# Output stores from SyncE's queue, and a new order of work, in a fused S4 convolution and SwiGLU kernel

## The chip, the cores and the metric

The kernel runs on one core of a Trainium2 chip, as one program. The metric is the device time of one execution in microseconds (us), as a median of runs. The core has TensorE (PE; its weight loads are shown as PEld), VectorE (DVE), ScalarE (ACT), GpSimd (POOL) and SyncE (SP), each with an instruction queue of its own that is worked off in order, and 16 DMA engines. DMAs are issued from SP's queue and, for some transfers, from ACT's; an engine issues a DMA as an instruction in its queue and does not wait for it to land.

## The reference

The input `x` (2048 rows of 512) is normalized row by row. Two branches start from the result: a state space convolution over the rows (S4: a filter of length 2048 for each of the 512 channels, made from 128 complex modes, applied through Fourier transforms) and a SwiGLU feed-forward layer (512 to 1792 to 512). The output adds their product to `x`.

```python
def _A_ref(u, A_re, A_im, B_re, B_im, C_re, C_im, log_dt, Dskip):
    ...
    P = jnp.exp(logdA[:, :, None] * l[None, None, :])
    K = jnp.einsum("dn,dnl,dn->dl", Cc, P, dB).real
    ...
    Yf = Uf * Kf[None, :, :, :]
    y = irfft2(Yf)[..., :L] + u * Dskip
def _B_ref(x, w_gate, w_up, w_down):
    g = _silu(x @ w_gate)
    u = x @ w_up
    return (g * u) @ w_down
x = A_u
xn = _layernorm(x, axis=-1)
s = _A_ref(xn, ...)
g = _silu(_B_ref(xn, ...))
return x + s * g
```

## The kernel before, in words

**A planner and a written-out order.** The kernel function does not emit instructions directly. It describes 1966 tasks by `add(engine, duration, function, rd, wr, up, ...)`: a task is one or a few instructions of one engine, with the buffers that it reads (`rd`), writes (`wr`) or fills a part of (`up`). The string `LIST` holds the order in which the tasks are emitted, two characters a task. `Plan.run` goes through the tasks in that order, gives each a time by its own durations, and from these times derives three things: where each buffer lies in one SBUF arena (`place`) and in eight PSUM banks, which DVE and POOL tasks are kept apart (`part_ports`), and where TensorE gets filler products while it would be idle (`keep_warm`, emitted at line 1439). Then the tasks' functions are called in list order; the framework adds the semaphores. So each engine works its own tasks in the order of the list, and the list sets the order of everything.

**The stages.** They overlap in the list.

- The head: `x_load`, `ln_group`, `x_norm` load tiles of `x` (xt), compute mean and rstd, centre and scale them, split them into two 16-bit parts (xh) and transpose them on PE (line 540, into xT). `w_load`, `w_norm`, `w_scale_gu`, `w_split` load the weights in chunks, square and sum them on ACT (line 604), and split each chunk into a high 16-bit part (ACT, line 669 or 666) and a low one (DVE line 670 or POOL line 667).
- The feed-forward layer: `half_mm` (line 699, 24 products of 256 columns a task, 16-bit) for gate and up, `ffn_unit` (ACT lines 720 and 724, DVE 722 and 725) and `down` (line 741, six products of 512 columns). SiLU of the result (zg, lines 750 and 753) is kept in SBUF, or for the first ten tiles in DRAM (zg_d).
- The filter: `prep`, `batch`, `kg_tables`, `kg_trig`, `kg_prod`, `kg_mm` (line 1150) and `kg_s1` (line 1183) make the filter and its first transform; it goes to DRAM as `ak_d`.
- The transforms: `x_stage1` (line 563) writes `ax_d`; `s2_load`, `s2_mm`, `s2_prod`, `s2_inv` load `ak` and `ax`, multiply them, transform back and write `bs_d` (DRAM, line 1295), for two halves of 256 channels.
- The end: `final` does the last transform of a pair of row tiles and one half of the channels, or of one row tile and all channels (the last two, 14 and 15). It loads `bt` from `bs_d` (by `load`, line 468), `fx` from `x` (line 1315), and for the first ten tiles `fz` from `zg_d`; PE makes `py` (line 1330), DVE multiplies by zg (1349 or 1337), DVE or POOL adds `fx` (1354, 1352 or 1338) and two DMAs store the result `ot`, one for each half of the partitions. A tag like `ot6_1` is the pair that begins with tile 6, second half of the channels; `bt15_1` is tile 15.

**Which queue stores.** A pair's two stores (128 KB each, 28 in all) are issued by ACT, and of the four stores of tile 14 and of tile 15 (64 KB each) two by SP and two by ACT:

```python
for h in range(2):          # tiles 14 and 15, line 1340
    add(("SP", "ACT")[h], 0.6, ... (sy, nc.scalar)[h].dma_start(ov[h, :, j0, sl], ot...), rd=[ot], ...)
...
for h in range(2):          # pairs, line 1356
    add("ACT", 0.6, ... nc.scalar.dma_start(ov[h, :, j0:j0 + nj, cs], vw(ot)...), rd=[ot], ...)
```

All other DMAs, but two halves of the first tiles of `x`, are issued by SP: 280 tasks of SP before.

Of the kernel before, what the change touches and what calls it, by code (L numbers as in the profile page):

```python
# [46 lines left out]
LIST = (
    "###$#(#'#%#&#K#J#L#)#D#T#.#M#i#k#l#U#V#W#Y#N#P#X#/&0#m#O#R#j#n#o#Z#Q#S#1#2#q(*#4#5#*#v#p#w#r#x&+#y(+(,#s$&(.#t#+"
    "$'#z$($)#{#[#,#-#](-${%Q#}#:$##_&A#d#^#e(/#|(0(4#f&3#`#8#g$*#a#;#b#7&.$-&/#C&:#<#h&1&,&5$$#c$}$.(:(6#9$w$x$1$y%%"
    "(1&B$+$z&?%.#?&z$2$3&;&<$/#=(5(7(<&=$=#0$<$;$4&6$,$>$5&D(@(8(L(9%&%'%<(F#A$6(;%$(A$F$?$Q$7(R#>$S$8$@%/$A#u%R$B$C"  # L50
    "$H&8$G(S$I$|(G%2$9(B$:(H(I(C(_(2$J$K#@$R$T(N(`#B(T&H(M#I&@#3$N$k%##6&F$b$U$L(D(=%T(O$V$M$Y$](X(>$D$E$%$O$P&G(e(3"
    "(J&9(P(U(Q(V(K#F(Y(Z(?([$0$^$W$X$Z$[(E&E&J(](^&V$e$n(W(g(a%($q$_$`(b%+$a$c#E(q&u(r(})#)$$t%7&C$f%8%9(k(f(w$g$d)("
    ")=)>(m%)(c(h(d(i)%%-%*%B%,)R)S&I$h%A(j%U&K)&(y$u%C(l$v$l$m%D$i(n&W%5$o$j$r)T(x$p)))0&k&X)1)?)F%E%Y%=%>(z%G%?$s&l"
    "%6&L&M&N&m&-({(|%0)U)2%F)]%H(o(p%:&a&b&c%1%@&Y%I%J)3%;(s%K-H)G%3%4%L%M&O&Z%N)H-I-M%O(t-N)I)'(u&d)J(v&e&n&o):);&P"
    ")^&4&Q&T&p&s&f&[&q-J-K&i-L&_&]-O-P&g&y'$-W%S-X&t-^)b)i)j)k-m)_)*-T-Q&j-Y&`-n&R-[-V-`-R)K-S)l-_-e-f)<-U)s)t)@-Z)+"
    "&v&})`-v&7-x-{&S)c-t-u&^-w-z-a&h-c),-b-g)B-i-d&2&>)A-h-q-o-s-p.6.7.8.9.:.;)a.<-])d-j)4&r.#.&.')-.%).)/)6)5#H)u.)"
    "-r)L)7.(.*-|.=%P-k-l-y)N)8.>)C)9-})D%Z&U.$.+.Y)E.A.C.?.@)V.B.F)w.H.K.D.E.G)x.,.-%V%`)W)M.../)v.I.1.J.L.M)m.0.2.3"
    "%a.Z.4.O)X.g)O.N.P.S)e.U)y)n.Q.R.[.T.5.]&w%[)o&x)f%d)g.h)h/$/%/&)Y)P)Q)p)z.c.p.^._.e.V.W.X)Z/#*$.`*%)[%W%X%n*1.i"
    ".j.l*2){)|.k.m.a.b/'/(*&*'*()q)r*.%].n/).o.d.q.r**%i*/.f.s%j%k*3/+)}.t.u*:*).v%_*+*,*4*#/*'#.w*0.y/./,/-%l*-.x.z"
    ".{%o%p*5%e&{%b%f*6/7/0/3/5%c.|.}&'%^%t*7/8*;*B//*C*F/F/1/9/2/:%s/4/<%m*<%u&|*8/;/=/S*=*G/6*D/H/I*E*9/G/@/>/B/?%v"  # L60
    "*H*I/T/A/M*>/N%w/K*L/P*M*N*?*O/l/m/n'%'S*@*A*T'&/k%q%r*J*P*Q*K/O/J/C/o/]/p*U*V&)*R/Z/[/L%y/U*S/Q/_/q/V*W/^/r*X%g"
    "/W'''(*Y/X0W')0Y*h/Y03'1'2/D/E*Z*]*^/t/u/R'3/`*['*'+/s/a/b'E'F'4'5*e*f/y*o%x/w/c/f/d%z%{*i0$#G';/g*j/e','/'-'6'9"
    "/z'7'0'G/h'./v*_':*`&#&$%|*k0%&%%}/x/{%h/}*l/|&*'T&&&(0@'80&*a'H*p'I'<'=0#040+0X0,*q*b0'0)*c*d*m*n/j'P0Z0A0.0D0-"
    "0709*w*x*r0(0*0/0F'O+$0B+%'>'?000<0>05+.06080[0:+/'J0C0E*s*g0;0=0I0K0102'U/i'M0]*t0^0_0G0H'@'A0`0a'C0b'D0c+00J'W"
    "*u*v0d+&'N0l0?0L*y0p0n110e0j0k0m'K0M0N+'+60g0i0f0h'V*z'Z0O0S'Y0Q0q*{1%0o0R0t0y0v0P0T+(+10w0x*|1$0z1:*}+#120{0V1+"
    "1,1.1&1'+)1(+2+3+4+50U1H1*+*+7+81)+++:0r0s0u0|1-'L1I+,1J1K'R'q1/10+-1314+>160}1#+9+;151L1M1N1P'Q'X'[18+?19+@171O"
    "+B'{+I'g1<+P1;+<+=1='B1Q1V1W1X1^1Y+A+C1]'h'i1>+Q1?+D1z1R1Z+X1T+Y1f1h+F1S'|'}'r's1U+a+G1@+H1D+J1B1l']'^'_1C1y1d1e"
    "1g'j(#'k1A1E1a($+b1m2627281_1c1`+L1{1|+R1b+E1n1o2#1G+K+M1p'`1['a1q25+N1i+O2''t2)'u+S+T1u1w1j1k1F1s1t'b+U+c29+d+Z"
    "1r+]'c2%2&2(1v+V+W2:1}2$2;2<'d2='v+['e'l(%2I2C2D'w1x'o'p(('y()2F2J2*+^2+2,+e2@2B2X2E2G(&2>2?2A(''z2Y+_'x'f+k+l+`"
    "+s2H2K2f+g'm'n2L2N2M2O2R+m+t2g3#2`+f2T2a2P3$2Q+h2b2Z2S2[2d2]2^2U2_+u2}2c3j3l+i+j+w2o3k2V+{2W2q2j2l2h2i+v2k+x3&3y"  # L70
    "3'2m3(+n2n2p2-2/213x+o+y+z3w+p2e2r483%2.20222423+q+r3m3}2s2t3p3n3o3r3q3t3)3s3z3*3{3|4#+|4%4&+}4$3u,#,(372u2w4'30"
    "4`,*,1,22v2x2y2z2{3v,$31334(2|3234363-3/3+3,3.,)384)4*3S,+,%4+,&,'474^3540413E,343443F464-4.393;4E3=3>3?3A3:3R,,"
    "3<4m,9,-3G3@,43H3J4/3B3L49,:,A3I3K,B3N3P3M3O4C4D3C3D3Y3V3X3Z3]4_3T4,3U3W4;3Q3[3^4<4:4=,.73,C4F4>4G4H4I4J4?5*4@4A"
    "4l3_3`3a4k4M4a454c4b,/,54B5,3b3c4L3e,;573d,<,03f3g593h424d4K4g4n4p4o4O4N,D5+4f,E,J,6,74h4e4j4P3i,8,K4Q4R5:4q4Z4["
    ",=585;4u4s4t4r5-,>4v4W4X4w5w,?,@,F,G4i4T4]4U5<5=5A5?4Y4S5.5/50545>5@5B,L,M,R5x6A4x,H5$4|52535Q51564y556(,N4z4{5%"
    "4V,S,T,O5',P6)5y5{5z,I4}5C5#,Q5(5|6$,U5)6B6*6,6+5&5^,Z,[6#6%5}6'6-606.6&616/626C6D6E,V72,W5R635S5T5_5U6F6H6J6G5`"
    "6I6K6g7X,X,Y5a,],^6h6N5b5D6L5H5I5J,e,l5E5F5G5N5O5P5K5L5M,m5c5f5g5e5d6i6j6k7V,t5h6M5i,c646t,d5V65667=67,f6s6>6?,g"
    "6O6Q6P5X5W6R5Y5Z5[5]6l6S6V6T6@6U6X6W,h8=7C71,_68696:6o6n6;6p6u6v6w6<7:74,u6m6r6=6x6|6z6{7L6y8+758)7F,|7G,n,i,j6q"
    "6}7W7i7#,`,},a8W7h,b765j7}7N-#,v7O,k5k5l7U,o5t5u5n7$5o5q5r5s5m7%7E8X7&,p847(7)7.,w7j777+6Y6Z7*7/7D7,7-6d,x6a7k6b"
    "6c6e6f-*-+7'8D6[5v7a6^-$5p,q70,r6]6_,y,z7r,s6`-,7_--7Y7Z7[82,{7P8E8:7`8c8(8;7]-.-/8f-08d7t7z-%-&-'8C-(-2-3-4-6-5"  # L80
    "-)8U817H-7-8-98V-17;7b787d8,7M7^7<-:8>8*7c7e-?7f8-7m7Q7I7K7q8<7s-@-A8N7J8?7R7>-;-<838e-=-B8L7?7@7B7|8F7S8H7T7l7n"
    "8G8@7{7o->8A8I8K8J8M-C8Y8Z8[7u8^-D-E-F85-G8_8#7g7v7p8O8.807A8B8/868`8b8a798P7w8Q8$7y7x87888g8h8]8i8k8l8j8m8o898n"
    "8R8S8T8%8&8'"
)
LIST = [DIGITS.index(a) * 90 + DIGITS.index(b) for a, b in zip(LIST[::2], LIST[1::2])]
ROOM = 103.0 * 1024
# [306 lines left out]
def kernel(  # L393
# [904 lines left out]
    def final(js, cs, c):  # L1298

        nj, nd = len(js), cs.stop - cs.start  # L1300
        j0 = js[0]
# [31 lines left out]
        if nj == 1:  # L1333
            for q, z in enumerate(zgs[j0]):
                ot = buf(f"ot{tag}{q}", 1024, "ot")
# [3 lines left out]
                for h in range(2):  # L1339
                    add(("SP", "ACT")[h], 0.6, lambda h=h, ot=ot, sl=sl: (sy, nc.scalar)[h].dma_start(ov[h, :, j0, sl], ot.f32()[h * 64:(h + 1) * 64]),  # L1340
                        rd=[ot], up=[key("out")], c=0, dma=dma_us(65536, 64), pr=pr)
            return
        ot = buf(f"ot{tag}", 2048, "ot", int(W["c_ot"] + 0.5))
        e = pr
# [8 lines left out]
        else:  # L1353
            add("DVE", 0.7, lambda: V.tensor_tensor(ot.f32(), ot.f32(), fx.f32(), op=ALU.add), rd=[fx], wr=[ot], c=1, pr=e, port=True)
        for h in range(2):
            add("ACT", 0.6, lambda h=h: nc.scalar.dma_start(ov[h, :, j0:j0 + nj, cs], vw(ot)[h * 64:(h + 1) * 64]), rd=[ot], up=[key("out")], c=0,
                dma=dma_us(131072, 64 * nj), pr=e)


# [127 lines left out]
```

## Time and profile before

| | |
|---|---|
| median of 3 runs | 598.75 us (598.53 to 599.48) |
| profiled execution | 597.17 us, its span 595.4 us |
| mean granted TensorE clock | 0.992 |
| PE busy | 578.9 us (97%), 7626 products |
| DVE, ACT, POOL busy | 428.6, 343.3, 325.8 us |
| DMA | 90.48 MB, mean 152 GB/s |
| queue of SP, of ACT | 85.12 MB, 4.20 MB |
| output stores: ACT line 1356, ACT 1340, SP 1340 | 28, 4, 4 |

How to read the views: the page's first part gives each engine's busy time; products on PE are pipelined, so a busy PE is not yet a PE at its peak. The stretches (a view by windows) give busy times, granted clock and DMA share in a part of the span. The chain of waits follows the work that ended last back from the end; a row is start, length and what it was. The timeline lists instructions in order of time, those of one kind merged (x5 is five of them, the second number the time that they took together); ACTq and SPq are DMA issues on the queue of ACT and of SP, and idle time before an instruction stands in brackets with what ended it. The view of one line gives the least, median and greatest duration in ns, and the time from a DMA's issue to its landing.

### The profile page before, as it was taken

How to read it: one execution, taken by the hardware profiler on the slowest of the kernel's cores; microseconds unless marked ns; L12 is line 12 of the kernel's file. 1: busy time of each engine (PE TensorE's matmuls, PEld its weight loads, DVE VectorE, ACT ScalarE, POOL GpSimd, SP SyncE). 2: the span in 40 equal slices, each digit the busy share in tenths (PEclk: the TensorE clock that was granted, in tenths of full speed). 3: DMA queues.
4: the chain of work that ended last, by engine and by line, in shares of the span. 5: the costliest groups of instructions: out<-in, count | busy, mean ns of one | idle time of the engine just before them, and what ended most of it. 6: DMA issues, size and time to landing. Idle time of an engine off the chain costs nothing.

```text
span 595.4 us, 18328 instructions
## 1 busy us (share of the span) xinstructions
PE 578.9 (97%) x7626; PEld 410.6 (69%) x7626; DVE 428.6 (72%) x992; ACT 343.3 (58%) x699; POOL 325.8 (55%) x301
## 2 busy tenths in 40 slices
...
GB/s 267 250 307 255 191 89 0 11 179 92 20 77 14 30 98 29 59 73 134 107 90 38 19 108 143 137 153 184 248 212 203 253 271 259 241 259 291 256 259 174
DMA packets 99762, 90.48 MB, mean 152 GB/s; under 512 B 38432, under 2 KB 84256, under 8 KB 99680
## 3 DMA queue, kind: packets, MB, share of 16 engines
q1 hardware_dynamic: 95168, 85.12, 49.5%
q10 hardware_dynamic: 4512, 4.20, 2.8%
...
## 4 chain that ended last, share of the span: by engine, by line
PE 92%; ACT 3%; issue 1%; DVE 1%; DMA 1%; SPq 0%; POOL 0%; POOLq 0%; ACTq 0%
PE p L699 48%; PE p L741 25%; PE p L1150 5%; PE p L1243 3%; PE p L1236 3%; PE p L1330 3%; PE p L1283 2%; PE p L563 1%; PE p L1183 1%; PE p L540 1%; DMA wd<-in_B_w_gate_dram 1%; ACT wu L604 1%; ACT wg L669 1%; PE p L799 1%; ACT wg L604 0%
## 5 line engine op out<-in xcount | busy, mean ns | idle before, releaser
L699 PE MATMUL p<-arena,wu 128*128 128x256 f16 x1344 | 154.7, 273 | 1.9 <-issue 1.8
L699 PE MATMUL p<-arena,wg 128*128 128x256 f16 x1344 | 155.0, 273 | 0.1
L741 PE MATMUL p<-wd,arena 128*128 128x512 f16 x672 | 154.2, 379 | 0.0
L699 PEld LDWEIGHTS <-wu 128*128 128x128 f16 x1344 | 130.0, 98 | 24.2 <-issue 7.5
L699 PEld LDWEIGHTS <-wg 128*128 128x128 f16 x1344 | 129.1, 98 | 25.0 <-issue 5.9
L741 PEld LDWEIGHTS <-arena 128*128 128x128 f16 x672 | 63.8, 98 | 73.8 <-issue 5.6
L1083 POOL TENSOR_TENSOR arena<-arena 128x1536 f32<-128x1536 f32 x32 | 90.7, 2842 | 25.4 <-ACT arena L720 6.2
L1075 POOL TENSOR_TENSOR arena<-arena 128x1024 int32<-128x1024 int32 x32 | 62.5, 1957 | 24.6 <-DVE arena L531 7.2
L720 ACT ACTIVATE arena<-p,inv 128x512 f32<-128x512 f32 x56 | 37.9, 685 | 46.3 <-PE p L699 41.3
L722 DVE SCALAR_TENSOR_TENSOR p<-p,shc,arena 128x512 f32<-128x512 f32 x56 | 41.9, 754 | 25.4 <-PE p L699 19.9
L724 ACT CAST arena<-p 128x512 f16<-128x512 f32 x56 | 32.5, 588 | 43.6 <-DVE p L722 40.4
L1118 DVE TENSOR_TENSOR arena<-arena,p 128x512 f32<-128x512 f32 x64 | 43.5, 680 | 6.3 <-ACT arena L567 2.6
L1265 POOL TENSOR_TENSOR arena<-arena 128x512 f32<-128x512 f32 x16 | 20.4, 1275 | 47.6 <-PE p L1236 14.3
L1098 ACT ACTIVATE p<-arena 128x512 f32<-128x512 int32 x64 | 38.7, 608 | 12.6 <-POOL arena L1075 5.6
L725 DVE TENSOR_TENSOR arena<-p,arena 128x512 f16<-128x512 f32 x56 | 37.7, 681 | 10.0 <-ACT arena L724 9.9
L1352 POOL TENSOR_TENSOR arena<-arena 128x512 f32<-128x512 f32 x12 | 15.0, 1268 | 51.5 <-DVE arena L1349 39.5
L1099 ACT ACTIVATE p<-p,halfpi 128x512 f32<-128x512 f32 x64 | 42.2, 664 | 1.5
L1100 ACT ACTIVATE p<-arena 128x512 f32<-128x512 int32 x64 | 37.6, 606 | 5.6 <-DVE arena L1120 3.2
L1124 DVE SCALAR_TENSOR_TENSOR arena<-arena,p 128x256 f32<-128x256 f32 x64 | 26.4, 413 | 18.7 <-POOL arena L1083 11.8
L1253 ACT COPY arena<-p 128x512 f32<-128x512 f32 x32 | 17.4, 591 | 31.0 <-PE p L1236 30.9
L1150 PEld LDWEIGHTS p<-arena 128*32 128x32 f32 x2048 | 29.7, 110 | 6.7 <-issue 4.4
L1150 PE MATMUL p<-arena 128*32 128x64 f32 x2048 | 33.6, 220 | 0.0
...
## 6 DMA issues: line engine op xcount, KB each, us to landing
...
ak_d<-arena SPq DMA_DIRECT2D x16, 512.0 KB, 5.8
arena<-ak_d SPq DMA_DIRECT2D x16, 512.0 KB, 4.5
arena<-ax_d SPq DMA_DIRECT2D x16, 512.0 KB, 5.2
...
arena<-in_B_w_down_dram SPq DMA_DIRECT2D x14, 512.0 KB, 6.0
arena<-bs_d SPq DMA_DIRECT2D x14, 512.0 KB, 6.4
```

The lines of the kernel that those rows point to most:

```text
L699: T.matmul(pg.t[:, i * 256:(i + 1) * 256].rearrange("p (a t) -> p a t", a=2), w[:, wl, d, i * P:(i + 1) * P], x[:, :, xl, d, :], start=(k ...
L720: add("ACT", 0.69, lambda: S.activation(sg.f32(), pg.t, AF.Silu, scale=inv[:, c, 0:1]), rd=[pg], wr=[sg], c=1, pr=e)
L722: add("DVE", 0.75, lambda: V.scalar_tensor_tensor(pu.t, pu.t, shc[:, c:c + 1], sg.f32(), op0=ALU.mult, op1=ALU.mult), rd=[sg], wr=[pu], c= ...
L725: add("DVE", 0.7, lambda: V.tensor_tensor(hh.view(F16)[:, 512:1024], pu.t, hh.view(F16)[:, 0:512], op=ALU.subtract), rd=[pu], wr=[hh], c=1 ...
L741: T.matmul(z.t, h[:, hl, i * 256 + t * P:i * 256 + (t + 1) * P], w[:, wl, i], start=(c == 0 and i == 0 and k == 0), stop=(c == NC - 1 and ...
L1075: G.tensor_tensor(a, h_[:, :, :, None].to_broadcast([P, 2 * GT, 4, 8]), l_[:, :, None, :].to_broadcast([P, 2 * GT, 4, 8]), op=ALU.add)
L1083: G.tensor_tensor(e, p_[:, :, :, None].to_broadcast([P, 3 * GT, 4, 8]), q_[:, :, None, :].to_broadcast([P, 3 * GT, 4, 8]), op=ALU.mult)
L1098: add("ACT", 0.62, lambda: S.activation(tc_.t, a(), AF.Abs, scale=SIN_SCALE), rd=[an], wr=[tc_], pr=pr)
L1099: add("ACT", 0.7, lambda: S.activation(tc_.t, tc_.t, AF.Sin, bias=halfpi, scale=-1.0), rd=[key("ones")], wr=[tc_], c=4, pr=pr)
L1100: add("ACT", 0.62, lambda: S.activation(ts.t, a(), AF.Sin, scale=SIN_SCALE), rd=[an], wr=[ts], pr=pr + 0.2)
L1118: V.tensor_tensor(o[:, :, 0:64].rearrange("p d (s j) -> p d s j", s=2), e[:, :, 0:64].rearrange("p d (s j) -> p d s j", s=2), t[:, :, None ...
L1150: T.matmul(kt[h * 32:(h + 1) * 32, (r * GD + dd) // 4], o[:, ri, dd + h, 64:96], o[:, ri, dd + h, 0:64], start=(ri == 0), stop=(ri == 1), ...
```

## The change

The two stores of a pair are issued by SP instead of ACT, and the list of work is another one. The tasks are the same 1966, with the same buffers; 28 of them change from ACT to SP, so that SP has 308 and ACT 558. Of the new list nearly every entry stands at another place: a task stands 16 places from its old one on average, 353 at most, of 1966. Taken by engine, TensorE's tasks move by 1.5 ranks on average, GpSimd's by 0.8, VectorE's by 2.8, ScalarE's by 3.7 and SyncE's by 8.6.

```diff
-LIST = "###$#(#'#%#&#K#J#L#)#D#T#.#M#i#k#l#U#V#W#Y#N#P#X#/&0#m#O#R#j#n#o#Z#Q#S#1#2#q(*#4#5#*#v#p#w#r#x&+#y(+(,#s$&(.#t#+"
+LIST = "###)#$#&#%#J#(#'#K#L#D#.#M#i#k#l#N#m#O#T#U#/#R#V#Y#j#1#P#W#n#o#S&0#v#q#Z#2#Q#X&+#p#w#5#x#y#4#+#*#-#s(*(+#r#z$'$&"
...
         for h in range(2):
-            add("ACT", 0.6, lambda h=h: nc.scalar.dma_start(ov[h, :, j0:j0 + nj, cs], vw(ot)[h * 64:(h + 1) * 64]), rd=[ot], up=[key("out")], c=0,
+            add("SP", 0.6, lambda h=h: sy.dma_start(ov[h, :, j0:j0 + nj, cs], vw(ot)[h * 64:(h + 1) * 64]), rd=[ot], up=[key("out")], c=0,
                 dma=dma_us(131072, 64 * nj), pr=e)
```

At the end of the list, TensorE's tasks stand as follows (a `down` z71 is the last row tile's; `py` names the `final` product):

```
before: ... py10_1, z71, py14_1, py0_1, z71, z71, py6_1, py2_1, py12_1, py15_1
after:  ... z70, py6_1, py14_1, py2_1, py12_1, py2_0, z71, z71, z71, py15_1
```

More of the change, by code (lines that the diff above doesn't have):

```diff
@@ L47 @@
 LIST = (
[L48 to L82, printed above, removed]
@@ new lines @@
+    "(U(J(K(P$t(`$%(9$F$0$Y&H%($Z(e$h$^%)$_(g&G(b&C(Q$n%*(q$[(Y$`([$a(]%7$c$d(}(f&>%8%9&V%S(^(c(d)$%+(k(m$l%-$m(V)R(W"
+    "&D(h(w%,)#(y&2&I$f(l)=&K%B$g&u&a%A%C%D$r(i&k(n$i(x)%$j$o)S%E)>)?)F%=&4)($s%>(o&l%F%Y(z))&W$p(r)T(p%G&L)0%0&M)1)G"
+    "&X({(j(|$u%1%H%:%;%5%I%J%K%?$v%L%M&b&c&m)H&N&Y%@)&)'(s-H#H-I%6-M-N&v&})U&d(t(u&/&Z&e(v%N)]%O%3%4)2)I)J)K&O)3&n&o"
+    "):&y&Q);&f&R&g&h&P&[&]&T&_&`&<&p-J&U&i&j)b)i&^-K-L-O-m-t-P&q&z-W)j)k&--T)^-^&s)*-u-g)+-Q)l)_-R-V-S&7)<-q-_-Y-n)`"
+    "-U&t)s)t)@)B-X-i-Z-[)a-{-o-p''-r%U)c-z)A-s-b-v-d.7-e.8-f-x#G),-`.9&r-a-c.6.:-]-h-j.;.<)4)C)6)d.#-w.%.&.'.(-k'$';"
@@ new lines @@
+    ")5.*.)-|-})L.=-l)D.>-y.$#I)-).)/)E)7%Z.?.@.F%P.B.+.Y.,.H)N)V.A.C.-)8)9)w.K)x.D.E&S.G%])u%V%`)M.J.../)m.I)O.0)W.L"
+    ")e.2%a.M.1.3.O)n.N.P.Z.Q)y.S.4.g)X)f%[.U.R)z.T.V%d)o)g)P)v)h.h){/$.W)Q.^/%/&.[.n.o.`)Y*$)Z.].5.X)p)q)[.c._)r.i.j"
+    ".e%W%X*1/#%i*2.l/'/(*%/).k*&*'*(.m*..a**.q.b.d.p*))|.r%n%j)}*#*+/+&{.f.s.t.u*3*:%b*/%k*0&x.v.w.y%o.x*4*5/*.z.{*6"
+    "%c.|/.%p%l%_/0/3/5.}%^%t%m*;/7/1*B/2/8/,*7/-//*C%e%f/4*F/F*</S%q/9/:%s/;&w/<&|/=*G*D*E/6/H/@/I%u%v/B*H%r*=*,*I*>"
+    "*-/>/?*L/A*M'%/M/N/G/T/l*8'#%w/C/m&)*9*N*P/P*?/K%y*@*A/J'&*T/L/k/o*U/O*O*Q*J*V*X'E/p/q/Q/]/U/V/_/Z/n*K/[/X*R*]/^"
@@ new lines @@
+    "*h/W*S*^/r*W*Y'('1')'2*Z/t/u/Y03'*/R/D/`/a*o*['3'4/s'+*e/E&'%x%z/b/c'5'F*f*g/f/d/w/e0$*i','/'6*_'0&#'7'8'9%{&$'-"
+    "/g/{0@/v/x%|/h*k%}%g&**`'G0W/y/z/|%h/}&%&&':0%*a*b0Y'<&(0Z'H'=*p0#04*q*j*l'.0&0'*c0)0(0X*m0A0**d0]0+0,0^0-0_*r0<"
+    "'I0D*n05060[0.0/*w*x+$'>0F'?'@/i0>000B0801'P*s0C0E+%'J0:0;02+.'C07'D+&+'+/*t*u0`090=0I0a0b0c0G0H*v+00K0d0J0?0L0p"
+    "'M*y'N+6'A0g0i'B0j0k0m'K'L0q0M0N0e0f0h0l0n+10O*{0S0t1%0v0P*z110Q0R0w*|0x0o1$'O'W+20y0{121I*}+(/j1J+#+71+1,1.'S+3"
+    "0r0s+)+41H1L'U0u+*0z0|'Q++1-1/+8+:0}1(+51*+,+-+>1K0T1&1'1)1:131<14161#1M1N1O+I1819+?+@1;+B+9+;'R15'X1]1P'V17'Z'T"
@@ new lines @@
+    "+<'Y+='g101=0U1S1Q'[1R1T1X1>+P+Q+X1^']+F1Z'^'h1V1?1W'i1z+A+Y1U1f1Y0V1h'{'|+C1@'q'}+J'_1y+a+G1d1e1D'r1g+D'j's1l1a"
+    "'k+b(#1A1C1B1E+H1m1_1`($+K261n271b28'`+L1o+R1c1{1|1q+M2#1F25291[1i'a+S+E't1p1r'u+N+O2'+c2)2:+T1u'b1G+Z+]1j+d2%2&"
+    "1k'e2(1s2;+U2<1w1}2$'c2=1t1v+[+V'f2C2D'v'y+W'l'z'o'p'm(%'n2I1x2*(&('((+^2F'w2f+e2@+g2>2J2B2?2A+_+k+l+s2E2G2P2+()"
+    "2,+f+h'x'd2X2K2L2Q2N2R2Y2M+`2T+m2`2b3l2g2Z2O2a3y2H2S3#2[2^2U2]2_2c2}3&+t+u+i+j+{+w+n2d3j2o2q3w3'2V2W3x2j2l2h2m+v"
+    "3$2i2-3%2n2k2p3k20+o+x2e2r2.+y212/22+p+q+z+r3m3(3*2s3}3o3p243n3s3q2t3z3)3|3t233{374#+|3r3u3v+}4E4%,#,(4$2u4&3-2y"
```

17 lines of the change are left out of this document (16 added, 1 removed).

## The prediction

> **What bounds the kernel now.** I read the page's first line for the engine that is never idle, then the stretches at both ends, then the chain of waits in the last 20 us, then the end instruction by instruction.
>
> ```profile
> span 595.4 us, 18328 instructions
> PE 578.9 (97%) x7626; PEld 410.6 (69%) x7626; DVE 428.6 (72%) x992; ACT 343.3 (58%) x699; POOL 325.8 (55%) x301
> ```
> ```profile
> 0.00:25.00 25.00, 23.73 (x158) 13.72 (x159) 17.02 (x62) 19.98 (x30) 2.63 (x6) 1.00 0.92 260
> ...
> 525.00:550.00 25.00, 25.00 (x315) 18.57 (x314) 12.03 (x27) 6.01 (x14) 1.27 (x1) 1.00 1.03 282
> 550.00:575.00 25.00, 25.00 (x159) 13.42 (x159) 9.55 (x17) 2.33 (x4) 5.67 (x5) 1.00 1.00 257
> 575.00:595.40 20.40, 7.25 (x50) 3.36 (x46) 7.36 (x14) 1.31 (x3) 6.84 (x6) 0.76 0.78 198
> ```
>
> Columns: stretch, length, busy PE, PEld, DVE, ACT, POOL, granted clock, DMA share, GB/s. TensorE is full from 25 us to about 582 us, so the middle gets shorter only if TensorE has less to do or waits less. The one long stretch without TensorE is the last: 7.25 us of 20.40. Who holds the end?
>
> ```profile
> 575.95 2.70 PE p L741 x12
> 578.65 3.55 PE p L1330 x27
> 582.19 0.25 DVE arena L1349
> ...
> 583.36 1.78 issue
> 585.14 1.29 POOLq L1482
> ```
> ```profile
> 577.35 2.27 ACTq L1356 DMA_DIRECT2D out_dram<-arena  x3
> ...
> 580.76 4.17 SPq L1340 DMA_DIRECT2D out_dram<-arena  x4
> ...
> 581.01 3.30 ACTq L1356 DMA_DIRECT2D out_dram<-arena  x5
> ...
> 584.35 0.68 DVE L1354 TENSOR_TENSOR arena<-arena 128x512 f32<-128x512 f32 x1
> ...
> 585.12 2.78 ACTq L1356 DMA_DIRECT2D out_dram<-arena  x4
> 585.17 1.26 POOL L1352 TENSOR_TENSOR arena<-arena 128x512 f32<-128x512 f32 x1 [1.81 <-issue]
> 588.00 1.21 ACTq L1340 DMA_DIRECT2D out_dram<-arena  x2
> 589.25 3.37 ACTq L1356 DMA_DIRECT2D out_dram<-arena  x5
> ```
> ```profile
> L1356 ACTq DMA_DIRECT2D out_dram<-arena x28: 602/617/928, 546.5 to 592.0; - x28
> ...
> L1340 SPq DMA_DIRECT2D out_dram<-arena x4: 466/497/596, 580.8 to 584.5; - x4
> ```
> ```profile
> DMA to landing us min/median/max: 2.4/2.5/7.6
> ...
> DMA to landing us min/median/max: 2.0/2.1/2.4
> ```
>
> The landing rows are those of lines 1356 and 1340. The chain loses its thread at 585 us (it ends in a wait at line 1482, the closing of the program), so the timeline has to say the rest. TensorE ends at 582.2, VectorE at 585.03, GpSimd at 586.43. ScalarE's queue goes on issuing output stores, one after another without a gap, until 589.25 + 3.37 = 592.62. The last starts at 592.0, lands 2.4 us later, and the program closes 1.0 us after that: 595.4. **The end is bound by the issue of stores on one queue**: 0.62 us each and, with what lies between two of them, one every 0.67 to 0.70 us (3.37 us for 5, 2.78 for 4), with about 17 stores unsent when TensorE stops (15 on ScalarE, 2 on SyncE). From TensorE's end to the program's end: 595.4 - 582.2 = 13.2 us.
>
> **Part 1, the end of the list.** Decoding both lists into tasks, the 28 stores of line 1356 go to SP, and the order is new. Before, the last four TensorE tasks are the `final` products of tiles 6, 2, 12 and 15, so their ten stores become ready only from about 581 on. After, tiles 6, 14, 2, 12 of the second half and 2 of the first stand ahead of the last three `down` tasks, and only tile 15 follows them. Take TensorE's end as 0 and walk SyncE's list backwards with the rows' times: 1.29 us a `down`, 0.91 to 1.01 a `final`, 0.7 + 1.27 us for a VectorE product and a GpSimd addition, a pace of 0.68 us for a store of 128 KB, and for SP 0.66 for half an `fx`, 0.58 for a larger load, 0.53 for a store of 64 KB (0.497 and a check of a semaphore).
>
> - The first store that SP can be held at is that of `ot6_0`. Its product ends at -20.2, VectorE at -19.3, GpSimd at -17.9: issue at -17.7.
> - With it and behind it stand 27 stores of 128 KB, 3 halves of `fx` (x for the residual), 3 larger loads and 4 stores of 64 KB. Back to back: 27 x 0.68 + 3 x 0.66 + 3 x 0.58 + 4 x 0.53 = 24.2 us. The second store waits 0.6 us for GpSimd's next addition (at -16.6). So to +7.1.
> - Tile 15's product ends at 0, and VectorE has its first half ready at about 2.2 and the rest by 3.0; its first store's turn comes at about 3.4: no wait. The last store is issued at 6.6, lands 2.1 later (64 KB), and the program closes 1.0 after that: **9.7 us after TensorE's end against 13.2: -3.5 us**.
> - ScalarE keeps four stores of 64 KB, issued by about 5: beside.
>
> The queue that the stores move onto is SP's, which also loads. What stands behind a store there: halves of `fx2_0` and `fx15_1`, `fz6_1`, both halves of `bt15_1`, half of `fx2_1`. By the walk the second half of `bt15_1` issues at -8.5.
>
> ```profile
> arena<-bs_d SPq DMA_DIRECT2D x14, 512.0 KB, 6.4
> ```
> ```profile
> 540.83 0.75 SPq L1295 DMA_DIRECT2D bs_d<-arena  x1
> ...
> 552.09 4.31 SPq L468 DMA_DIRECT2D arena<-bs_d  x5
> ```
>
> With 5 us from issue to landing it is there at -3.5, and its product starts at -0.9: a cover of 2.6 us. The other narrow place is `bt4_1`: the last store of `bs` (before: issue at 540.83, 41.4 us ahead of TensorE's end) must land first, then the load takes the 6.4 us of the row; I get -27.6 for a product that wants it at -26.7. Bytes: 11.1 MB follow the last `bs` store in the new list (11.6 MB in the old). At the 265 GB/s between the two rows of 525 to 575 us that is 42 us from -40, to +2: the DMA engines are full but not late.
>
> **Part 2, TensorE's order.**
>
> ```profile
> 192.80 2.59 PE p L741 x12
> ...
> 203.85 2.70 PE p L741 x12
> ```
> ```profile
> 562.66 3.99 PE p L741 x18
> 566.66 1.01 PE p L1330 x8
> 567.67 3.99 PE p L741 x18
> ```
>
> Twelve `down` products are 2.59 us after another 16-bit task and 2.70 us after one of 32-bit tiles (line 1150 before 203.85), and eighteen are 3.99 after line 1330, against 1.5 x 2.59 = 3.88. A change of the kind of tile costs 0.10 to 0.11 us. Counting neighbours of different kind (the f32 number in `add`) along the two lists: 140 before, 126 after. 14 x 0.10 = **-1.4 us**; nothing covers it, TensorE being full, and nothing is late instead unless an input is (next part).
>
> **Part 3, the head.** Here TensorE waits for ScalarE and VectorE.
>
> ```profile
> 11.01 1.13 ACT L669 ACTIVATE wg<-wd,scw 128x1024 f16<-128x1024 f32 x1
> ...
> 17.24 1.13 ACT L669 ACTIVATE wg<-wd,scw 128x1024 f16<-128x1024 f32 x1
> ...
> 19.80 2.11 PE L1439 MATMUL p<-ones 128*128 128x512 bf16 x9
> ...
> 21.44 1.28 DVE L670 SCALAR_TENSOR_TENSOR wg<-wd,scw,wg 128x1024 f16<-128x1024 f32 x1
> 21.74 2.96 PE L699 MATMUL p<-arena,wg 128*128 128x256 f16 x24
> ...
> 27.05 2.79 PE L699 MATMUL p<-arena,wg 128*128 128x256 f16 x24
> ```
>
> The new list centres tile 1 of x after the square of the first `w_gate` chunk, not before (0.7 us of ScalarE moved into the chain), and converts that chunk after one more square (1.0 us): the conversion at 11.01 comes at about 12.8, the one at 17.24 at 18.0. In return VectorE's low part of chunk 1 (21.44) stands ahead of the second group's rstd and can start near 19.2, so the 2 us of filler products at 19.80 mostly go. But the transposes of tiles 2 and 3 then wait for the centring behind ScalarE's SiLU. My walk brings the task of 27.05 to 27.8, with 0.2 us less TensorE work ahead of it: **+0.9 us**, with an uncertainty of 1.5 either way, as it adds a dozen small steps.
>
> **Part 4, the middle.** By list position every task of the filter generation and of the two transforms stands within a few us of where it stood; the smallest leads of the `ak` and `ax` loads grow from 3.3 and 4.2 us to 6.4 and 7.5. Zero; bound: one wait of the size that shows there now, gained or lost.
>
> ```profile
> 435.19 2.03 PE L699 MATMUL p<-arena,wu 128*128 128x256 f16 x17 [1.79 <-issue]
> ```
>
> TensorE stands 1.79 us in the midst of one task with nothing to wait for that the profile shows.
>
> **Sum.** The profiled execution took 597.17 us (span 595.4 and 1.8 around it). 597.17 - 3.5 - 1.4 + 0.9 = 593.2. The median of the three runs, 598.75, lies 1.6 above that execution, so **594.8 us**.
>
> **Rivals.**
> 1. *SyncE becomes the bound (slower).* The stores leave a queue that did little else and enter the one that loads. Row 1356 has a median of 0.617 and a maximum of 0.928 us. If beside loads a store costs near the maximum, 27 x 0.31 = 8.4 us more lie on SP: 603.2 us, with the second `bt15_1` late too. It decides from about 0.2 us more per store on (27 x 0.2 = 5.4 us, which lifts 594.8 to 600.2). Against it: SP's own 128 KB loads in the same stretch issue at the same pace, and the 19 stores of ScalarE's rows above kept theirs. The Trainium skill (DMA: Bandwidth & Descriptors, Issuing engines are not separate DMA queues) says that issuing on several engines saves only sequencer time, usually small beside the transfer; by that rule this change gives up the only thing a second queue brings. The trace differs on "small": 0.62 us a store, with 128 KB at 257 GB/s taking 0.5 us, is what ends this kernel.
> 2. *The end is won, TensorE loses part.* `bt4_1` or `bt15_1` late by 2 to 4 us in a full DMA system, or the head worse: 596.8 to 598.8.
> 3. *More is won.* Head equal, the stop of 1.79 us gone: 594.8 - 0.9 - 1.8 = 592.1 us.
> 4. *Nothing is won.* DMA stays the bound: at 0.78 the last 20 us have 4.5 us of DMA time free, little more than the 3.5 I claim of them. If the bytes come as late as before: 598.
>
> **How the numbers follow.** Forecast (593.3 to 596.3, 1.5 us either way) 0.46, rival 3 0.16, rival 2 0.16, rival 4 0.06, rival 1 0.16. Over 0.2% (1.2 us, about what a measurement of this kernel can tell from no change) faster: 0.46 + 0.16 + 0.12 of rival 2 = 0.74; same: the rest of rival 2 and rival 4, 0.10; slower 0.16. The range takes in rivals 2 and 4, and below rival 3 the 1.5 us by which the head may differ: 590.6 to 598.8.
>
> **What would show it.** Right: ScalarE's queue with four stores of line 1340 only; SP's stores unbroken from some 18 us before TensorE's end to 7 us after it; from TensorE's last product to the end 9 to 10.5 us; the `down` after `final` pieces fewer. Wrong: SP issues at 0.8 us or more; gaps of TensorE before line 1330; more than 12 us after TensorE's end; the task of 27.05 later than 29.

## The result, and the profile after

The changed kernel takes 606.84 us (603.35 to 607.27, three runs) against 598.75: a ratio of 1.0113 (1.0084 to 1.0142). It is slower by 8 us where 4 us less were forecast. Its profiled execution is the quickest of its three, 603.35 us with a span of 601.6 us, against 597.17 and 595.4 before: 6.2 us of the loss can be followed in the traces. Among the executions of the experiments below, one of e3_half_stores took 1203.7 us, twice the others, and is left out of its ratio.

First line and engines of the page of the changed kernel:

```profile
span 601.6 us, 18303 instructions
PE 578.3 (96%) x7625; PEld 411.8 (68%) x7625; DVE 431.8 (72%) x992; ACT 342.9 (57%) x699; POOL 326.6 (54%) x301
```

TensorE is busy no longer than before (578.3 against 578.9), in a span that is 6 us longer: it waits more. The waits of TensorE in the kernel before, then in the changed one (us in total, times, longest):

```profile
PE p L699 <- issue: 1.8, 1, 1.8
PE p L1439 <- DVE halfpi L474: 1.1, 1, 1.1
PE p L1243 <- issue: 0.2, 1, 0.2
```

```profile
PE p L1243 <- issue: 4.6, 2, 2.4
PE p L615 <- DVE hsq L614: 1.4, 3, 0.8
PE p L1330 <- DMA arena<-bs_d: 1.1, 2, 0.9
PE p L1439 <- DVE halfpi L474: 1.1, 1, 1.1
PE p L540 <- DVE arena L531: 0.4, 1, 0.4
```

The first row is the large one: twice, at 394 and 433 us, TensorE stands over 2 us in the middle of a task with nothing to wait for that the profile shows. It is the kind of stop that the prediction saw once and put at zero. The third row is a late `bt` tile. The changed kernel's timeline of SyncE at the end:

```profile
569.72 2.25 SPq L1356 DMA_DIRECT2D out_dram<-arena  x3
572.34 1.27 SPq L1315 DMA_DIRECT2D arena<-in_A_u_dram  x2
574.91 0.36 SPq L468 DMA_DIRECT2D arena<-zg_d  x1
577.12 1.30 SPq L1356 DMA_DIRECT2D out_dram<-arena  x2
...
584.87 8.93 SPq L1356 DMA_DIRECT2D out_dram<-arena  x13
...
597.83 1.21 SPq L1340 DMA_DIRECT2D out_dram<-arena  x2
```

SyncE starts its stores where the walk had them (569.72 is 17.5 us ahead of TensorE's end at 587.2; the walk said 17.7), but has gaps up to 577, and is then busy to 599.0. From TensorE's end to the program's end it takes 14.4 us, not 9.7, and not the 13.1 of before.

To split the 6.2 us I took each TensorE task's time to the next one, less what such a task takes elsewhere in the trace and 0.10 us where the kind of tile changes. What is left are stops (us); filler products that ran in place of work, and stretches in which TensorE ran at a lower clock, count in them too:

| | first product | stops to 35 us | 35-380 | 380-450 | 450-550 | from 550 | changes of kind | TensorE's end | from there to the end |
|---|---|---|---|---|---|---|---|---|---|
| before | 9.30 | 5.02 | 0.21 | 3.33 | 0.26 | -0.16 | 140 | 582.25 | 13.14 |
| after | 10.46 | 6.02 | 0.10 | 6.10 | 0.73 | 0.90 | 126 | 587.20 | 14.36 |
| difference | +1.16 | +1.00 | -0.11 | +2.77 | +0.47 | +1.06 | -1.40 | +4.95 | +1.22 |

The last two entries of the difference add up to the 6.2 us; the others add up to TensorE's 4.95. The first product's 1.16 is chance: the first chunk of `w_gate` landed at 9.04 us in this execution, at 7.66 before, and of the kernels below those with the new head have their first product at 8.9 to 10.1 us, those with the old head at 9.1 to 9.8.

### The profile page after: what moved, and what is told of

Read it like the earlier page. It is cut to its first block, busy times and chain, and to the rows that moved or that the text cites. A ratio compares the mean times of both kernels' runs of the same rounds, so it can differ in the third digit from the quotient of the medians.

```text
span 601.6 us, 18303 instructions
## 1 busy us (share of the span) xinstructions
PE 578.3 (96%) x7625; PEld 411.8 (68%) x7625; DVE 431.8 (72%) x992; ACT 342.9 (57%) x699; POOL 326.6 (54%) x301
## 4 chain that ended last, share of the span: by engine, by line
PE 90%; issue 2%; DVE 2%; DMA 2%; SPq 1%; ACT 1%; POOL 1%; DVEq 0%; POOLq 0%; ACTq 0%
PE p L699 49%; PE p L741 23%; PE p L1150 5%; PE p L1243 3%; PE p L1236 2%; PE p L1283 2%; PE p L563 2%; PE p L1183 1%; PE p L540 1%; DMA wd<-in_B_w_gate_dram 1%; PE p L1330 1%; POOL arena L1352 1%; SPq L1356 1%; PE p L799 1%; DMA out_dram<-arena 0%
## 5 line engine op out<-in xcount | busy, mean ns | idle before, releaser
L1352 POOL TENSOR_TENSOR arena<-arena 128x512 f32<-128x512 f32 x12 | 15.4, 1299 | 50.0 <-DVE arena L1349 29.0
L1266 POOL TENSOR_TENSOR arena<-arena 128x512 f32<-128x512 f32 x16 | 20.4, 1275 | 37.2 <-DVE arena L1261 19.6
L1265 POOL TENSOR_TENSOR arena<-arena 128x512 f32<-128x512 f32 x16 | 20.4, 1278 | 31.3 <-DVE arena L1261 30.4
```

## The experiments

All kernels, in the columns of the table above; the ratio is to the kernel before, run on the same chip. "Both" means one of a pair's two stores on SP, one on ScalarE; "old+new 1600" is a list that follows the old order for its first 1600 tasks. Stops and the time after TensorE's end are of one profiled execution; the executions of one kernel spread by 1.4 to 6.3 us.

| run | list | pair stores | fillers cut in | stops 380-450 | from 550 | after TensorE's end | median us | ratio |
|---|---|---|---|---|---|---|---|---|
| e1_stores_alone | old | SP | 1 | 3.07 | -0.17 | 16.1 | 600.5 | 1.0037 (1.0019-1.0054) |
| e2_list_alone | new | ScalarE | 1 | 7.79 | 1.15 | 17.8 | 607.75 | 1.0153 (1.0120-1.0185) |
| e3_half_stores | old | both | 1 | 2.48 | -0.16 | 10.4 | 594.53 | 0.9935 (0.9899-0.9971) |
| e4_code_gaps | new, 5 tasks moved | SP | 1 | 11.05 | 1.51 | 13.2 | 607.84 | 1.0153 (1.0126-1.0180) |
| e5_new_end | old+new 1600 | SP | 1 | 2.17 | 2.81 | 13.2 | 599.51 | 1.0014 (0.9996-1.0032) |
| e6_old_end | new+old 1600 | ScalarE | 1 | 7.71 | 1.41 | 15.6 | 602.91 | 1.0070 (1.0041-1.0099) |
| e7_code_phase | new | SP | 2 | 1.24 | 4.33 | 13.9 | 598.14 | 0.9982 (0.9963-1.0001) |
| e8_old_loads | new, SP's 46 old | SP | 1 | 10.07 | 2.81 | 14.3 | 609.86 | 1.0186 (1.0153-1.0220) |
| e9_new_list_half_stores | new | both | 1 | 6.62 | 2.37 | 13.0 | 603.62 | 1.0091 (1.0059-1.0124) |
| e10_phase_half_stores | new | both | 2 | 1.44 | -0.37 | 11.9 | 597.29 | 0.9966 (0.9948-0.9985) |
| e11_old_list_phase | old | both | 2 | 2.18 | -0.20 | 11.5 | 598.9 | 0.9999 (0.9975-1.0022) |
| e12_code_phase_full | new | SP | 4 | 8.70 | 1.10 | 13.9 | 605.68 | 1.0123 (1.0102-1.0143) |
| e13_half_bytes | new | SP, half of each | 2 | 1.43 | 2.81 | 14.4 | 598.04 | 0.9991 (0.9974-1.0009) |
| e14_old_end_phase | new+old 1600 | both | 2 | 2.19 | -0.16 | 10.8 | 595.11 | 0.9940 (0.9919-0.9960) |
| e15_old_ends_phase | old 500, new to 1600, old | both | 2 | 0.90 | -0.08 | 12.1 | 593.38 | 0.9906 (0.9883-0.9929) |

**A lower clock after some stops.** Not all of a stop in this table is waiting. The granted clock is 1.00 from the first products to past TensorE's end in the traces of the kernel before and of the changed one. In seven others it falls to 0.50 once on the way, during a stop or within 1.4 us of its end: for 3.4 us in e2, e6, e8 and e12 (between 396 and 444 us), in e15 (from 526.7) and in e7 (from 566.9, behind a late tile), and for 10.2 us in e4 (from 404.3). There TensorE's work takes longer. In e4, 18 `down` products take 6.98 us, against 3.99 in the row of 562.66 in the prediction:

```profile
408.53 6.98 PE L741 MATMUL p<-wd,arena 128*128 128x512 f16 x18 [0.56 <-DVE arena L1263]
```

Half of such a stretch is lost. By this estimate 1.7 us of each of 7.79, 7.71, 10.07 and 8.70 us between 380 and 450 us (e2, e6, e8, e12) are clock, and so are some 5 of e4's 11.05 and 1.7 of e7's 4.33 from 550 us on.

**Queue or list.** The change has two parts that can be had apart. The stores alone (old list, only line 1356 changed):

```diff
-            add("ACT", 0.6, lambda h=h: nc.scalar.dma_start(ov[h, ...], vw(ot)[...]), ...)
+            add("SP", 0.6, lambda h=h: sy.dma_start(ov[h, ...], vw(ot)[...]), ...)
```

> The old list, with line 1356 on SP: the queue changed alone. Theory (one queue is too little: SP has at most eight DMAs in flight, so stores and loads hold each other up, and the stores come out at 0.65 us each): the first 395 us as before; TensorE 0 to 3 us later at the end by late loads, TensorE's end to program's end 13 to 15 us; 599 to 603 us. Rival (the queue costs nothing, the new order does it all): 598.75 within 1 us, with 13 us after TensorE's end.

The list alone (the new `LIST`, line 1356 left with ScalarE):

> The new list, with line 1356 on ACT as before: the order changed alone. Theory (head and code fetch lose some 5 us, the queue the rest): TensorE's end within 1 us of the changed kernel's 587.2, or 1 us earlier as loads no longer stand behind stores; the time after it 8 to 11 us instead of 14.4; 600 to 603 us. Rival (the order itself loses everything): 605 to 608 us, 14 us after TensorE's end.

And the old list with the two stores of a pair on two queues:

```diff
-            add("ACT", 0.6, lambda h=h: nc.scalar.dma_start(ov[h, ...], vw(ot)[...]), ...)
+            add(("SP", "ACT")[h], 0.6, lambda h=h: (sy, nc.scalar)[h].dma_start(ov[h, ...], vw(ot)[...]), ...)
```

> The old list, with one of a pair's two stores on SP and one on ACT. Theory (the end of before is bound by the issue on ACT alone): TensorE's end unchanged at 582 us, the time after it 8 to 10 us instead of 13.2; 594 to 596 us. Rival (the end is bound by the DMA engines or by the data): 598 to 599 us.

The queue alone costs 0.4%, the list alone 1.5%: most of the loss is the list's. Neither queue alone is good at the end (16.1 us with SP, 13.1 with ScalarE, old list), two queues are: 10.4 us, 594.5 us, less than either kernel. With the new list, ScalarE is a bad place for all the stores, as the timeline of the list alone shows:

```profile
590.49 0.47 ACT L750 ACTIVATE arena<-p,zsc 128x256 f32<-128x256 f32 x1 [5.92 <-DMA out_dram<-arena]
...
596.50 0.47 ACT L750 ACTIVATE arena<-p,zsc 128x256 f32<-128x256 f32 x1 [5.54 <-DMA out_dram<-arena]
```

ScalarE's SiLU of the last row tiles stands behind stores in its queue, and VectorE waits for it with tile 15's product. So that list needs the stores elsewhere; moving them to SP shortens its end from 17.8 to 14.4 us and is no gain by itself (the ratios, 1.0153 and 1.0113, have intervals that overlap).

**Which part of the list.** The lists are joined at task 1600 (at about 478 us in both traces; the text below says 458):

```diff
-LIST = NEW
+LIST = OLD[:1600] + [t for t in NEW if t not in OLD[:1600]]      # e5; e6: OLD and NEW exchanged, stores on ScalarE
```

> The old order for the first 1600 of the 1966 tasks (to about 458 us), the new order for the rest, all pair stores on SP. Theory 1 (the new end brings nothing by itself: SP's backlog after TensorE's end is as long as ScalarE's was, and the late tiles stop TensorE for 1.5 us): TensorE's end within 1.5 us of 582.3, 13.5 to 16 us after it, time 1 to 3 us above the kernel before (599 to 601). Theory 2 (the end is worth the predicted 3.5 us and was only eaten by the lateness of the middle): tail near 9.7 us, 594 to 595. Head and stops at 393 and 432 us as in the kernel before in both.

> The new order for the first 1600 tasks, the old order for the rest, pair stores on ScalarE as before: the new list's head and middle alone. Theory 1 (the new list loses in the head, 1 us, and by TensorE's stops at 393 and 432 us, 3 to 4.5 us, less 0.9 us for 9 fewer changes of tile kind): 601 to 603, stops of 6 to 8 us between 380 and 450 us, tail near 13. Theory 2 (those stops are chance, the loss belongs to the new end): 597 to 599 with stops of about 3 us.

The new end, with its stores on SP, is no gain (1.0014; it gets TensorE's stops on late `bt` tiles, 2.8 us, for its fewer changes of kind); the new head and middle alone cost 0.7%, with the same two stops near 393 and 433 us as the changed kernel. By the time Theory 1 of both held (599.5 and 602.9 us), but not in every term: TensorE ended at 585.1 us in e5, 2.8 us later than before where at most 1.5 were expected, and e6 took 15.6 us after TensorE's end where 13 were.

**What the stops are.** One row of the page of the changed kernel (its DMA queues: packets, MB, share of the 16 engines) matters here:

```profile
q8 instruction: 60, 0.98, 0.7%
```

Queue 8 brings 60 packets, 0.98 MB: 16 KB each, and with 7625 products and 7625 weight loads about 254 of TensorE's instructions to a packet. In every stop of over 2 us, TensorE starts again 2.2 to 2.8 us after a packet of that queue has begun. And before and after break off the same task at the same product (kernel before, then changed kernel):

```profile
391.74 1.05 PE L1243 MATMUL p<-arena 64*32 64x256 f32 x27
393.02 1.27 PE L1243 MATMUL p<-arena 64*32 64x256 f32 x35 [0.22 <-issue]
```

```profile
393.18 1.05 PE L1243 MATMUL p<-arena 64*32 64x256 f32 x27
396.37 1.27 PE L1243 MATMUL p<-arena 64*32 64x256 f32 x35 [2.14 <-issue]
...
432.28 0.61 PE L1243 MATMUL p<-arena 64*32 64x256 f32 x8
435.30 1.07 PE L1243 MATMUL p<-arena 64*32 64x256 f32 x24 [2.41 <-issue]
```

So TensorE seemed to run out of code at the end of a block, in runs of small products (lines 1150, 1236, 1243: 128 or 256 instructions in some 2 us, where a task of line 699 has 48 in 2.8 us). The first try was to break up those runs with `down` and `half_mm` tasks:

```diff
-LIST: ..., s2_mm, s2_mm, s2_mm, s2_mm, ..., down, down, ..., half_mm, ...
+LIST: ..., down, half_mm, s2_mm, s2_mm, down, s2_mm, s2_mm, ...   # 5 TensorE tasks moved
```

> The changed kernel, with five of TensorE's long 16-bit tasks moved some places ahead, so that they part the runs of short 32-bit tasks (kg_mm, s2_mm) near 393 and 432 us in which TensorE stands 2.45 and 3.03 us. Theory (it stands because its code is fetched in blocks of 256 instructions, and a run of short ones is through a block before the next is there): both gone or under 0.7 us, 601 to 604 us. Rival (it waits for data, the products of the filter or the loads of ak and ax): the stops stay, at the same tasks, 606 to 608 us.

It says nothing on the code: the stops at line 1243 went, but the moved tasks' readers and writers on the other engines kept their places, and waits for data came instead, with 10.2 us at half clock behind one of them. The planner also put five filler products at 391 us, which shifts the code by 10 instructions. The first rows of TensorE's waits on VectorE and on DMAs in it:

```profile
PE p L1236 <- DVE arena L1167: 1.9, 1, 1.9
PE p L1330 <- DMA arena<-bs_d: 1.7, 1, 1.7
```

The clean way leaves every task alone and shifts the code under it. While TensorE is idle in the head it runs 44 filler products; cut into two or four, each brings more instructions and no more work:

```diff
-        return lambda: T.matmul(bank... , ones, ones[:, None, :].to_broadcast([P, 4, P]), start=True, stop=True)
+        return lambda: [T.matmul(bank...[:, k:k + 2], ones, ones[:, None, :].to_broadcast([P, 2, P]), start=True, stop=True) for k in (0, 2)]
```

> The changed kernel with each of its 44 filler products cut into two of half the width, in the idle time of the head: 88 more TensorE instructions (product and weight load) ahead of the middle, no more work. Theory 1 (TensorE stands because the next 16 KB block of its code, 256 instructions, comes late): the stops at 393 and 432 us come at the same instruction numbers as before (9629 and 10899 of TensorE), which is 88 instructions, some 44 products, earlier in the work; the first gets about 1.3 us shorter, the second may move to another block; total 604 to 608. Rival (the stop waits for data of those two tasks): the same tasks stop for the same 2.4 and 3.0 us, at instruction numbers 88 higher, 603 to 607.

> The changed kernel with each of its 44 filler products cut into four of a quarter of the width: 264 more TensorE instructions in the idle head, which is one block of code (256) and 8. Theory (what counts is where the ends of the blocks fall in the runs of short products): the stops come back as in the changed kernel, 5 to 8 us between 380 and 450 us, at the products of lines 1243 and 1150, 603 to 608. Rival (the gain of the kernel with halved fillers came from something else that smaller fillers do, in the head or the clock): stops stay at 1 to 2 us, 596 to 600.

With 88 instructions more both stops are gone, but for one of 0.7 us at another place. That is better than Theory 1 had it (598.1 us against 604 to 608): it expected some 1 us to stay at the first place, and nothing did. With 264 more, a block and 8, they are back. Timeline of TensorE around 393 us, halved fillers first, then quartered:

```profile
391.74 2.06 PE L1243 MATMUL p<-arena 64*32 64x256 f32 x64
```

```profile
393.15 1.04 PE L1243 MATMUL p<-arena 64*32 64x256 f32 x23
396.34 1.29 PE L1243 MATMUL p<-arena 64*32 64x256 f32 x37 [2.16 <-issue]
...
432.27 0.60 PE L1243 MATMUL p<-arena 64*32 64x256 f32 x4
433.44 1.08 PE L1243 MATMUL p<-arena 64*32 64x256 f32 x28 [0.57 <-issue]
```

The break comes after 23 products of line 1243 and not 27, after 4 and not 8: four products, that is 8 instructions, earlier in the work, exactly the 8 by which 264 exceeds 256. The time follows: 598.1 us in phase, 605.7 out of it. A wait for data cannot do that.

Counting shows the same in every trace. Take all of TensorE's instructions, with the semaphore waits and the like that stand among the products and weight loads (84 to 92 in all). Then every stop of 0.45 us or more after 36 us that the profile puts to "issue", 32 of them in sixteen traces, begins after instruction 8641, 9665, 9921, 10945, 11201, 11457 or 14529. Each of these numbers is 193 above a multiple of 256. The stops for data (late `bt` tiles, e4's waits for VectorE) begin at other remainders. So all kernels pass the same places, and what differs is how long TensorE stands there: at 9665 it is 0.2 us before and 2.1 us in the changed kernel, at 11201 it is 1.8 us and nothing.

The Trainium skill (Runtime: NRT & Kernel Launch, Instruction fetch mechanics) states the blocks of 16 KiB and 256 instructions, which the trace agrees with, and calls the cost of crossing from one to the next mostly hidden; here the long stops are 2.1 to 3.2 us each, and 7.5 us lie between the two medians.

Why a block comes in time or not was the next question. The packet of a block that stops TensorE begins some 400 instructions past the block's multiple of 256, most others 100 to 300 past it: it comes late, not only TensorE early. Rival causes were SP's transfers around it:

```diff
-LIST = NEW
+LIST = NEW with SP's 46 tasks of 355 to 450 us in the old order, each beside the TensorE task of the old list
```

> The changed kernel, with SyncE's 46 transfers between about 355 and 450 us put back into the old order and beside the TensorE task that they stood beside in the old list; the other four engines keep the new order. Theory 1 (the code block comes late because it stands behind a burst of data transfers that the new order bunches up): stops between 380 and 450 us fall from 6.1 to about 3.3 us, total some 2.5 us below the changed kernel. Rival (the runs of short products in TensorE's new order alone outrun the code): stops stay at 5.5 to 8 us, total as the changed kernel.

Theory 1 failed, and the run decides little: stops rose to 10.1 us, but this list also got 60 fillers in place of 44 from the planner. The 16 more run from 430.8 us on, count as stops themselves, and move the code's phase by up to 32 instructions from there. Ahead of them the stop at 394 us stands at the same instruction and is 1.3 us long instead of 2.1, in one execution. What makes a block late stays open.

**The end.** If one queue is too slow and the code is in phase, both mended should win:

> The changed kernel's list, with the two stores of a pair on SP and on ScalarE instead of both on SP. Theory (the end is long because one queue has at most eight DMAs in flight, so that each issue waits for the landing of the eighth before it; two queues carry sixteen): TensorE's end as in the changed kernel, 586 to 588, 10 to 11 us after it instead of 14.4, time 599 to 602. Rival (the stores on ScalarE hold up its SiLU of the last tile, as they did with all stores there): 13 us or more after TensorE's end, 603 to 607.

> The new list with the stores of a pair on SP and ScalarE, and each filler product cut into two (88 more TensorE instructions in the idle head). If the two losses are what was found (late blocks of code in the middle, eight DMAs in flight of one queue at the end), both go: stops of 1 to 2 us between 380 and 450 us, TensorE's end at 580 to 582, 10 to 11 us after it, 592 to 595, below both kernels. Rival (the end is bound by the bytes that the DMA engines carry, so that whatever TensorE gains it waits for late bt tiles): stops of 3 to 4 us after 550 us again, 596 to 598.

> The old list with the stores of a pair on SP and ScalarE (594.5 us before this) and each of its 45 filler products cut into two, 90 more instructions. If the new list is better by itself (14 fewer changes of tile kind, 1.4 us) once the code comes in time in both, this one ends 1 to 2 us later than the same with the new list: 593 to 596; stops between 380 and 450 us between 1 and 3 us. Rival (the old list is as good or better): 590 to 592, below the new list's.

Two queues shorten the new list's end too, from 14.4 to 13.0 us, less than the theory and as much as the rival had, because ScalarE's SiLU of tile 15 again stands behind stores. With the code in phase as well it is 597.3 us, below both kernels, by less than expected; its profiled execution (593.8 us) has nearly what was expected, no stops after 550 us, TensorE's end at 580.1 us and 11.9 us behind it, but the median of its ten runs is 3.5 us above. The old list does not gain by the shift (598.9 us against 594.5, above both forecasts): it gets a new stop, 1.4 us at line 1283 at 526 us, in another block. A shift suits one order and not another.

Whether SP is held by issuing or by landings was told apart by halving the bytes of its stores:

```diff
-... sy.dma_start(ov[h, :, j0:j0 + nj, cs], vw(ot)[h * 64:(h + 1) * 64]) ...
+... sy.dma_start(ov[h, :, j0:j0 + nj, cs.start:cs.start + HD // 2], vw(ot)[h * 64:(h + 1) * 64, :, :HD // 2]) ...
```

> The changed kernel with halved fillers (code in phase, all pair stores on SP: 598.1 us, 13.9 us after TensorE's end, 4.3 us of TensorE's stops on late tiles after 550 us), each of its 28 pair stores writing only the first half of its columns: as many issues and as many rows, half the bytes; the other half of the output stays unwritten. Theory 1 (SP is held by landings: at most eight DMAs in flight, so its pace is that of the bytes): the stores land sooner, SP's waits in the last 30 us go, the stops after 550 us fall to 1 us or less, and 9.5 to 11 us pass after TensorE's end: 591 to 594. Rival (SP is held by the 0.6 us of each issue, as the prediction's walk had it): SP's last issue as far behind, 13 to 14 us after TensorE's end, stops as before: 596 to 599.

The rival held for the stores: with half the bytes 14.4 us pass after TensorE's end, the stops from 550 us on are 2.8 us (against 4.3, of which 1.7 were clock), and DMA is far from full. Stretches of this kernel (the last columns are granted clock, DMA share, GB/s):

```profile
575.00:585.00 10.00, 7.85 (x48) 3.49 (x44) 4.75 (x11) 0.84 (x2) 3.79 (x3) 1.00 0.54 144
585.00:590.00 5.00, 0.00 (x0) 0.00 (x0) 1.38 (x4) 0.00 (x0) 0.00 (x0) 0.62 0.49 116
```

and its stores still go at one per 0.65 us for the most part, 13 in 8.91 us:

```profile
580.25 8.91 SPq L1356 DMA_DIRECT2D out_dram<-arena  x13
```

What the walk lacked is in the waits of SP's queue, in the changed kernel from 569.7 us on:

```profile
SPq L1356 <- DMA arena<-bs_d: 2.1, 2, 1.8
SPq L1482 <- DMA out_dram<-arena: 1.4, 1, 1.4
SPq L468 <- DMA arena<-bs_d: 1.2, 1, 1.2
SPq L1356 <- DVE arena L1349: 0.5, 1, 0.5
SPq L1315 <- DMA arena<-in_A_u_dram: 0.4, 1, 0.4
SPq L1356 <- POOL arena L1352: 0.3, 1, 0.3
```

Without line 1482, the program's closing, that is 4.5 us. A store (line 1356) reads nothing of `bs_d`, yet waits for the landing of a load from there. The landings say why: the issue at 577.12 comes 0.06 us after the landing of the eighth DMA before it, and so do those of 569.72, 571.37, 572.34 and 574.91 (0.01 to 0.06 us). The trace's record of each instruction's semaphores says what holds them. All DMAs of this program, SP's and ScalarE's together, tell of their landing by the same eight semaphores, taken in turn, and ahead of an issue the queue waits for the semaphore that the new DMA is going to use. So a DMA waits for the landing of the eighth before it, whichever of the two queues issued that one. In the traces in which every landing is known (before, after, e9, e10, e15) never more than eight DMAs are under way in both queues together. These waits are instructions of the program, added by the framework like all its semaphores; no run here shows a limit of a queue itself. The kernel's planner has such a limit written in, for each engine apart (`flight[e][-8]` in `Plan.run`). So e9's theory that two queues carry sixteen DMAs does not hold here. What a second queue gains is, as far as the traces show, that two stores are issued at a time: in e3 both queues issue from 578 to 588 us. In the DMA-full stretch to 575 us the loads of `bt` took 9 to 10 us to land, and held the stores behind them; with stores of half the bytes the wait is nearly the same (2.0 and 1.4 us).

**Towards a better one.** The new end brings late tiles, the new head costs 1 us, the new middle saves changes of kind; so the old end, then the old head too, with the code in phase and stores on both queues:

> The new list to task 1600, the old one after it, the stores of a pair on SP and ScalarE, halved fillers. Theory (the new end brings late tiles and nothing else, the new middle saves 9 changes of tile kind, 0.9 us, once its code comes in time): no stops after 550 us, 1 to 2 us between 380 and 450 us, 10.4 us after TensorE's end as with the old list: 592 to 594.5. Rival (late code again, elsewhere): a stop of 1.5 to 3 us at another place, 596 to 598.

> The old list for the first 500 tasks (the head), the new one to task 1600, the old one after it; the stores of a pair on SP and ScalarE, halved fillers. Theory (the old head is worth 0.5 to 1 us): 0.5 to 1 us less than the same with the new head, 591.5 to 594. Rival (the head makes no difference that shows beside the phase of the code, which moves by two instructions): equal within 0.5 us.

Both are faster than before and after, the second the fastest of all, 593.4 us (0.9906). But e3_half_stores, the old list with two queues alone, has nearly the same (0.9935, with an interval that overlaps those of both), so no run shows that the new middle or the shift adds anything to the second queue. The late tiles are gone; a new stop of 1.6 to 1.9 us for code stands near 526 us, so there is some left. What the head is worth is not settled (the two medians lie 1.7 us apart, with intervals that overlap).

## Why the prediction was wrong, point by point

- **Part 1, the end: failed.** That the end of the kernel before is bound by the issue of stores on one queue was right: with two queues it is 10.4 us instead of 13.1 (e3). But forecast for one queue on SP were 9.7 us after TensorE's end, and measured 14.4. The pace of a store was right (13 in 8.93 us, 0.69 each, against 0.68), the first store's time was right (17.5 us ahead against 17.7), the count was right. The step that failed is "back to back": 4.5 us of waits stood in SP's list, 3.7 of them for earlier DMAs, and the last issue came at +11.2 and not at +6.6. The walk checked when data were ready and when SP was free, but not whether the semaphore of the next DMA was, that is, whether the eighth DMA before it had landed.
- **`bt` late (rival 2's mechanism): came true.** Tiles 8 (`bt8_1`, which the prediction did not name) and 15 stop TensorE for 1.0 and 0.25 us. The second half of `bt15_1` was issued 5.4 us ahead of TensorE's end and not 8.5, held up like the stores, and that is more than its cover of 2.6 us. The price, 1.1 us, lies below the rival's 2 to 4.
- **Part 2, changes of kind: right by count**, 140 to 126; the sum closes with -1.4 us.
- **Part 3, the head: right in size.** Forecast +0.9, measured +1.0 us in the stops of one execution. ScalarE's two conversions (forecast at 12.8 and 18.0) came at 14.18 and 19.38, both 1.4 us behind, as much as the first chunk of `w_gate` landed later. Part 3's own sign of being wrong showed all the same: the task of 27.05 came at 29.23, later than 29, because the first product's 1.16 us of chance came on top.
- **Part 4, the middle: failed, and worth most of the loss** (2.8 of 6.2 us; against its own forecast Part 1 is further off, by 4.7 us). Forecast zero, bounded by one stop of 1.8 us; measured +2.8 us in this execution and +4.5 with the list alone, of which some 1.7 are clock. The prediction had the row of the stop in its hands (1.79 us, waiting for nothing that the profile shows) and took it for something that stays or goes by chance. It belongs to a place in the code (instruction 11201 in the count above), so a new order puts other work at all such places at once: two long stops instead of one.
- **Rival 1**, SyncE as the bound, named the right engine with a wrong price: stores beside loads issue at a median of 0.603 us, no dearer than on ScalarE, and SP is late all the same. The Trainium skill's rule quoted there (DMA: Bandwidth & Descriptors, Issuing engines are not separate DMA queues) speaks of a small saving; here, with the old list, one queue more is worth 6.0 us (600.5 to 594.5). The trace differs.
- **Rival 3** ("the stop of 1.79 us gone") is what halved fillers do, but at 598.1 us and not 592.1: the end's loss is left over.
- The medians add some 2 us to what the profiled executions show (8.1 against 6.2); the two other runs of the changed kernel have spans of 605.1 and 605.5 us and no trace. Their granted clock is lower, 0.988 and 0.985 against 0.991. One and two stretches of 3.4 us at half clock, as in the traces of e2 or e12, would make that difference (an estimate: half of 3.4 us is 0.003 of the span). In e6 the executions divide that way: three with a clock of 0.992 took 600.2 to 602.3 us, five with 0.986 to 0.989 took 602.9 to 605.9. For the changed kernel it is not shown.
